# The MLP of the last two batches as 2x2 blocks with seven block products

## The chip, the cores and the metric

The kernel runs on one core of one Trainium2 chip. The metric is the device time of one execution in microseconds; three executions of the kernel before gave a median of 391.68 us (391.42 to 391.88).

## The reference

Attention with one added to the softmax denominator, then an MLP with a squared ReLU, in numpy (cut):

```python
batch, n_heads, seq, head_dim = (8, 12, 448, 64)
scores = scale * np.matmul(q, k.transpose(0, 1, 3, 2))
m = np.max(scores, axis=-1, keepdims=True)
e = np.exp(scores - m)
attn = e / (np.sum(e, axis=-1, keepdims=True) + np.exp(-m) + 1e-09)
attn_out = np.matmul(attn, v)
x = attn_out.transpose(0, 2, 1, 3).reshape(8 * 448, 12 * 64)     # 3584 x 768
h = x @ w_in                                                     # 768 x 2048
r = np.maximum(h, 0.0)
out = (r * r) @ w_out                                            # 2048 x 768, float32
```

Inputs and output are float32; the kernel works in fp16 with float32 sums in PSUM.

## The kernel before

**Layout.** `x` of a batch lies transposed in SBUF as `xts[b]`, six chunks of 128 features by 448 tokens. `win` holds w_in as six chunks of 128 by 2048, `wout` holds w_out as sixteen chunks (`fb`) of 128 by 768. `gs` holds the squared activations, transposed: sixteen blocks of 128 hidden features by a ring of 896 tokens, that is two batches.

**Order.** The kernel writes out the order of every engine's instructions by hand: each engine runs its queue in the order in which the Python code issues it. The string `ORDER` does the first four batches' attention and the beginnings of the MLP, the string `CYCLE` (L750) is run twice, for `b` = 4 and 6 (L774). A run with `b` = 6 does the attention of batches 6 and 7 and, between its steps, the MLP of batches 4 and 5 that lags behind. In these strings `s` computes scores, `e` their exponentials on ScalarE, `a` sums of exponentials on VectorE, `S` the denominators on TensorE, `Z` and `M` their reciprocals on ScalarE, `v` the product with the values, `X` (`quad_x`, L482) the scaled result into `xts`; `o` is a part of an output tile (`out_piece`), `O` and `Q` its two reads from PSUM on VectorE or ScalarE and the store on SyncE's queue; `d` issues DMAs on POOL's and SP's queues.

**PSUM.** Two pools matter: `s_psum` (L61) has two tiles named `sp` of `[128, 2, 512]` float32, each two banks; the ring (`mp_tile`, L86) has four tiles named `mp` of one bank each. The tile framework adds semaphore waits so that a write into a tile comes after the reads of it that were issued earlier, and a read after the writes.

**The last stage**, after the two cycles, is a plain loop. For each of the batches 6 and 7 and each of 16 blocks of hidden features, `tile_in` (L781) issues six matmuls of 128x448 into one `mp` tile, one read with ReLU on VectorE (L505) and one square on VectorE into `gs` (L509). Then `tile_out` (L787) does the output of their 896 tokens, 128 tokens by 384 columns at a time: sixteen matmuls into one `mp` tile, one scaled read on ScalarE (L575) and the store. The last 384 columns are done as 256 and 128.

Of the kernel before, what the change touches and what calls it, by code (L numbers as in the profile page):

```python
# [16 lines left out]
def kernel(  # L17
# [62 lines left out]
    vns, qks, xts, naturals, stages = {}, {}, {}, {}, {}  # L80
# [5 lines left out]
    def mp_tile(dtype=FP32):  # L86
        return ring[-1].tile([128, 512 if dtype == FP32 else 1024], dtype, name="mp")
# [4 lines left out]
    def mm(out_, lhsT, rhs, start, stop):  # L92
        return nc.tensor.matmul(out_, lhsT, rhs, start=start, stop=stop)  # L93
# [69 lines left out]
    def transposed_load(b, i):  # L163
        qk = qk_of(b)
        n, x, c = PLANES[i]
        nc.sync.dma_start(
            out=qk[:, i, 0:c],
            in_=stages[n, b][x:x + c * 2 * D].rearrange("(r c) -> r c", c=2 * D),
            transpose=True,
        )  # L170
# [329 lines left out]
    def relu(hp, key, m, act):  # L500
        rt = rts[key] = r_pool.tile([128, 512], FP16, name="rt")
        if act:
            nc.scalar.activation(out=rt[:, 0:m], in_=hp[:, 0:m], func=AF.Relu)  # L503
        else:
            nc.vector.tensor_scalar(out=rt[:, 0:m], in0=hp[:, 0:m], scalar1=0.0, scalar2=None, op0=ALU.max)  # L505

    def squared(key, t0, n, f0, per):
        r = rts.pop(key)[:, 0:per * n].rearrange("p (j n) -> p j n", j=per)
        nc.vector.tensor_mul(gs[:, f0:f0 + per, t0 % RING:t0 % RING + n], r, r)  # L509
# [3 lines left out]
    def later_in(b, f0, c0, c1, cols=False):  # L513
        if c0 == 0:
            hps[b, "all", f0] = mp_tile()
        hp, xt = hps[b, "all", f0], xts[b]
        for dc in range(c0, c1):
            product(hp[:, 0:S], win[:, dc, f0 * 128:(f0 + 1) * 128], xt[:, dc, :],
                    start=(dc == 0), stop=(dc == DCH - 1), cols=cols)

    def later_relu(b, f0, act):
        relu(hps.pop((b, "all", f0)), (b, "all", f0), S, act)

    def later_squared(b, f0):
        squared((b, "all", f0), S * b, S, f0, 1)
# [69 lines left out]
    raw = load_first_quad()  # L595
# [113 lines left out]

    def period(b):
        m = NQ * (b - 1)
        first = EARLY + 2 * KC * (b - FIRST_PERIOD) // 2

        def following(n):
            ahead, what = ((1, n) if n < 6 else (2, 6) if n < 7 else (1, 6) if n < 8 else (2, n - 8))
            t = b + ahead
            if t < B and (n != 7 or b > FIRST_PERIOD):
                if what < 3:  # L720
                    transposed_load(t, what)
                elif what < 5:
                    tail_keys(t, (what - 2,))
                elif what == 5:
# [7 lines left out]
        return {  # L732
            "s": lambda x, c: quad_scores(m + x, c),
            "e": lambda x, c: quad_exp(m + x, c),
            "a": lambda x, step: add_quad(m + x, step),
            "S": lambda x: sums_of_quad(m + x),
            "Z": lambda x: quad_z(m + x),
            "M": lambda x: quad_reciprocal(m + x),
            "v": lambda x, c: values_step(m + x, c),
            "X": lambda x: quad_x(m + x),  # L740
            "j": lambda n, c0, c1: later_in(*block(n), c0, c1, True),
            "k": lambda n, act: later_relu(*block(n), act),
            "l": lambda n: later_squared(*block(n)),
            "o": lambda n, f0, f1: out_piece(128 * ((first + n) // 2), HALF * ((first + n) % 2), HALF, range(f0, f1), True),
            "O": lambda n, act: out_first(128 * ((first + n) // 2), HALF * ((first + n) % 2), HALF, act),
            "Q": lambda n: out_second(128 * ((first + n) // 2), HALF * ((first + n) % 2), HALF),
            "d": lambda n: following(n),
        }

    CYCLE = """  # L750
# [11 lines left out]
        v0,5 M0 v0,6 s2,2 s2,4 o5,0,2 o5,2,4 o5,4,6 o5,6,8 e2,2 a1,0 o5,8,10 s2,0 e2,4 X0 a1,1 e2,0 o5,10,12 o5,12,14 s3,1 o5,14,16 e3,1 o6,0,2 a1,2  # L762
        a2,0 s3,4 o6,2,4 o6,4,6 O5,0 e3,4 o6,6,8 Q5 s2,5 o6,8,10 o6,10,12 s1,6 e2,5 o6,12,14 e1,6 o6,14,16 a2,1 s3,2 a1,3 o4,0,2 d3 o4,2,4 o4,4,6
        e3,2 s2,6 e2,6 O6,0 o4,6,8 S1 a2,2 Z1 o4,8,10 Q6 o4,10,12 a2,3 o4,12,14 o4,14,16 s3,5 v1,0 O4,0 Q4 v1,1 M1 v1,2 v1,3 v1,4 e3,5 v1,5 v1,6 S2
        v2,0 Z2 v2,1 v2,2 v2,3 v2,4 v2,5 v2,6 X1 M2 o7,0,2 s4,3 e4,3 s3,3 o7,2,4 o7,4,6 X2 e3,3 o7,6,8 o7,8,10 o7,10,12 o7,12,14 o7,14,16 O7,0 Q7 s3,0
        s4,2 e3,0 o8,0,2 o8,2,4 o8,4,6 a3,0 o8,6,8 s3,6 o8,8,10 e4,2 o8,10,12 o8,12,14 e3,6 o9,0,2 s4,1 o8,14,16 s4,0 o9,2,4 O8,0 d10 e4,1 Q8 e4,0
        o9,4,6 o9,6,8 s4,6 o9,8,10 o9,10,12 o9,12,14 s4,4 o9,14,16 e4,6 e4,4 s4,5 d8 o10,0,2 a4,0 o10,2,4 o10,4,6 a3,1 O9,1 d12 a3,2 e4,5 Q9 o10,6,8
        o10,8,10 s5,4 o10,10,12 o10,12,14 s5,1 e5,4 a3,3 o10,14,16 e5,1 a4,1 o12,0,2 O10,0 s5,0 Q10 d9 o12,2,4 d11 e5,0 o12,4,6 s5,5 e5,5 a4,2 o12,6,8
        o12,8,10 o12,10,12 a4,3 s5,3 o11,0,2 o11,2,4 o12,12,14 o12,14,16 e5,3 s5,2 o11,4,6 S3 e5,2 O12,0 o11,6,8 Q12 o11,8,10 o11,10,12 Z3 o11,12,14
        s5,6 o11,14,16 v3,0 O11,1 v3,1 v3,2 v3,3 v3,4 a5,0 v3,5 S4 v3,6 Q11 a5,1 o13,0,2 M3 X3 o13,2,4 o13,4,6 o13,6,8 o13,8,10 o13,10,12 o13,12,14  # L770
        o13,14,16 Z4 a5,2 e5,6 a5,3 O13,1 v4,0 M4 v4,1 v4,2 Q13 v4,3 v4,4 v4,5 v4,6 S5 v5,0 v5,1 v5,2 Z5 M5 v5,3 v5,4 v5,5 X4 v5,6 X5 d13
    """

# [5 lines left out]
    done = EARLY + 2 * KC * (B - FIRST_PERIOD) // 2

    def tile_in(b, f0):  # L781
        for c in range(0, DCH, 2):
            later_in(b, f0, c, c + 2)
        later_relu(b, f0, False)
        later_squared(b, f0)

    def tile_out(tok, n0, w):  # L787
        out_piece(tok, n0, w, range(NFFB))
        out_done(tok, n0, w)

    tiles = [(128 * (n // 2), HALF * (n % 2), HALF) for n in range(done, NT // 64 - 1)]
    tiles += [(NT - 128, HALF, 256), (NT - 128, HALF + 256, 128)]
    for b in (B - 2, B - 1):
        for f0 in range(NFFB):
            tile_in(b, f0)
    for t in tiles:
        tile_out(*t)
# [1 line left out]
_INS = ['q', 'k', 'v', 'moe_w_in', 'moe_w_out']  # L799
_OUTS = [((3584, 768), 'float32')]  # L800
# [25 lines left out]
```

## Time and profile before

| | |
|---|---|
| median of three executions | 391.68 us (391.42 to 391.88) |
| span of the profiled execution, first to last instruction | 389.7 us |
| TensorE, VectorE, ScalarE busy | 382.2, 251.9, 228.4 us |
| last stage: in products | 313.89 to 350.22 us |
| last stage: out products | 350.22 to 386.82 us |
| granted TensorE clock | 1.000 |

No separate time of the profiled execution itself is listed; its span is 2.0 us below the median of the timed ones. In the lines of the profile PE is TensorE, PEld its weight loads, DVE VectorE, ACT ScalarE, POOL GpSimd, SP SyncE; a group reads: line, engine, operation, output <- inputs, shapes, count, then busy time and mean nanoseconds of one, then the idle time in front of them and what ended it. A matmul's mean there is longer than its share of the stream, since consecutive ones overlap; what a matmul costs in a stream is read from windows.

### The profile page before, as it was taken

Reading aid. Unit: us, or ns where it says so; the run is one execution under the profiler, and the core shown is the slowest. Engines: PE = TensorE matmul, PEld = TensorE weight load, DVE = VectorE, ACT = ScalarE, POOL = GpSimd, SP = SyncE. Lnnn points to the kernel's source line nnn. Section 1 sums busy time; section 2 is a strip of 40 time slices with the busy share of each in tenths; the row PEclk is TensorE's granted clock in tenths of the full one; section 3 lists DMA queues with packets and bytes.
Section 4 is the critical chain, followed back from the end, with each engine's and each line's share of the span. In section 5 each row is a group of like instructions: output and inputs, shape, how many; then the busy total and the mean of one; then the engine's idle time right before and its main releaser. Section 6 shows DMA issues by size and latency. Waiting matters only on the chain.

```text
span 389.7 us, 14257 instructions
## 1 busy us (share of the span) xinstructions
PE 382.2 (98%) x6432; PEld 255.2 (65%) x6432; DVE 251.9 (65%) x468; ACT 228.4 (59%) x308; POOL 61.3 (16%) x96
## 2 busy tenths in 40 slices
PE   9789999999999999999999999999999999999997
PEld 5566656566789765667777655567777755556665
DVE  2987994765666766547958757466878788880000
ACT  5999998586689512259988731248988720001221
POOL 8543420025000603100001241210000000000000
DMA  9999999999939899802229697901112200001132
GB/s 154 203 204 205 200 201 204 189 179 176 213 80 150 180 210 203 92 3 65 44 64 202 139 188 160 148 6 47 61 44 64 64 23 2 0 0 62 61 82 81
DMA packets 75052, 45.34 MB, mean 116 GB/s; under 512 B 47472, under 2 KB 72944, under 8 KB 74992
## 3 DMA queue, kind: packets, MB, share of 16 engines
q0 software_dynamic: 24752, 22.62, 37.5%
q1 hardware_dynamic: 49952, 21.59, 27.9%
q8 instruction: 50, 0.82, 0.9%
q10 hardware_dynamic: 288, 0.23, 0.2%
q14 instruction: 10, 0.08, 0.1%
HBM read 45.69 MB, written 17.93 MB: 163 GB/s over the span
## 4 chain that ended last, share of the span: by engine, by line
PE 93%; ACT 4%; DVE 1%; issue 1%; DVEq 0%; ACTq 0%
PE mp L93 81%; PE sp L93 9%; ACT et L254 3%; PE xp L93 2%; PE mp L207 1%; ACT rcp L372 1%; PE mp L234 0%; DVE qk L217 0%; ACT rcp L365 0%; DVE half L341 0%; DVE half L347 0%; ACT rcp L368 0%; DVE half L343 0%; ACT rt L503 0%; DVE half L345 0%
## 5 line engine op out<-in xcount | busy, mean ns | idle before, releaser
L93 PE MATMUL mp<-wout,gs 64*64 64x384 f16 (+2 forms) x2928 | 165.6, 322 | 0.0
L93 PE MATMUL mp<-xt,win 128*64 128x448 f16 (+2 forms) x1188 | 148.3, 347 | 0.1
L93 PEld LDWEIGHTS <-gs 64*64 64x64 f16 (+1 forms) x2928 | 104.3, 106 | 33.6 <-issue 0.2
L93 PEld LDWEIGHTS <-win 128*64 128x64 f16 (+1 forms) x1188 | 83.2, 106 | 63.4 <-issue 4.1
L254 ACT ACTIVATE et<-sp 128x896 f16<-128x896 f32 (+2 forms) x131 | 110.5, 889 | 11.9 <-PE sp L93 11.5
L505 DVE TENSOR_SCALAR rt<-mp 128x448 f16<-128x448 f32 x87 | 54.1, 622 | 16.8 <-PE mp L93 13.8
L509 DVE TENSOR_TENSOR gs<-rt 128x448 f16<-128x448 f16 x128 | 48.3, 395 | 22.1 <-ACT rt L503 20.3
L503 ACT ACTIVATE rt<-mp 128x448 f16<-128x448 f32 x41 | 21.8, 543 | 64.9 <-PE mp L93 55.6
L575 ACT ACTIVATE ot<-mp 128x384 f32<-128x384 f32 (+2 forms) x31 | 14.9, 480 | 70.3 <-PE mp L93 70.0
L93 PE MATMUL sp<-qk 64*64 64x224 f16 (+1 forms) x1056 | 53.9, 274 | 2.2 <-DVE qk L217 0.8
L93 PEld LDWEIGHTS <-qk 64*64 64x64 f16 x1056 | 33.1, 114 | 15.0 <-issue 6.6
L188 POOL COPY flatq<-qk 64x384 f16<-64x384 f16 x20 | 13.8, 690 | 170.8 <-DMA qk<-stage_k 139.5
L254 ACT ACTIVATE nn<-sp 128x896 f16<-128x896 f32 x42 | 37.1, 916 | 4.2 <-PE sp L93 4.2
L487 DVE TENSOR_TENSOR xt<-mp,rcp 128x448 f16<-128x448 f32 x42 | 24.3, 619 | 15.7 <-ACT rcp L466 12.1
L581 DVE SCALAR_TENSOR_TENSOR ot<-mp,ot 128x384 f32<-128x384 f32 x42 | 23.4, 557 | 13.8 <-ACT ot L575 11.3
L93 PEld LDWEIGHTS <-vn 64*64 64x64 f16 x756 | 22.5, 107 | 9.4 <-issue 1.0
L93 PE MATMUL mp<-et,vn 64*64 64x448 f16 (+1 forms) x448 | 24.4, 343 | 0.0
L577 DVE TENSOR_SCALAR ot<-mp 128x384 f32<-128x384 f32 x26 | 14.4, 555 | 15.1 <-PE mp L93 14.9
L463 ACT ACTIVATE rcp<-sp,one_b 128x896 f32<-128x896 f32 x21 | 21.2, 1007 | 3.2 <-PE sp L93 3.1
L466 ACT ACTIVATE rcp<-rcp 128x896 f32<-128x896 f32 x21 | 19.9, 948 | 0.5
L441 DVE TENSOR_TENSOR half<-et 128x1792 f16<-128x1792 f16 x15 | 16.4, 1090 | 4.3 <-ACT et L254 4.2
L443 DVE TENSOR_TENSOR half<-half,et 128x1792 f16<-128x1792 f16 x15 | 16.3, 1087 | 0.3
(59 smaller groups left out, 195.9 us busy)
## 6 DMA issues: line engine op xcount, KB each, us to landing
out_dram<-ot SPq DMA_DIRECT2D x52, 96.0 KB, 2.6
out_dram<-ot SPq DMA_DIRECT2D x19, 192.0 KB, 1.9
win<-in_moe_w_in_dram POOLq DMA_DIRECT2D x8, 384.0 KB, 11.9
wout<-in_moe_w_out_dram POOLq DMA_DIRECT2D x4, 768.0 KB, 15.0
vn<-in_v_dram POOLq DMA_DIRECT2D x10, 288.0 KB, 8.0
stage_q<-in_q_dram POOLq DMA_DIRECT2D x4, 676.0 KB, 11.1
stage_k<-in_k_dram POOLq DMA_DIRECT2D x4, 676.0 KB, 13.8
nn<-in_q_dram POOLq DMA_DIRECT2D x8, 224.0 KB, 8.2
```

Source lines behind the costliest of these rows:

```text
L93: return nc.tensor.matmul(out_, lhsT, rhs, start=start, stop=stop)
L254: nc.scalar.activation(out=out_, in_=in_, func=AF.Exp, scale=scale)
L441: nc.vector.tensor_add(esq[m], a[:, 0:w], a[:, w:2 * w])
L443: nc.vector.tensor_add(esq[m], esq[m], z[:, 0:w])
L463: nc.scalar.activation(out=rcp, in_=zp[:, :, 0:S], func=AF.Ln, bias=one_b)
L466: nc.scalar.activation(out=zqs[m], in_=zqs[m], func=AF.Exp, scale=-1.0)
L487: nc.vector.tensor_mul(xts[b][:, 2 * g + i, :], xqs[m][i][:, 0:S], zqs[m][:, i, :])
L503: nc.scalar.activation(out=rt[:, 0:m], in_=hp[:, 0:m], func=AF.Relu)
L505: nc.vector.tensor_scalar(out=rt[:, 0:m], in0=hp[:, 0:m], scalar1=0.0, scalar2=None, op0=ALU.max)
L509: nc.vector.tensor_mul(gs[:, f0:f0 + per, t0 % RING:t0 % RING + n], r, r)
L575: nc.scalar.activation(out=ot, in_=op[:, 0:w], func=AF.Copy, scale=OUT_SCALE)
L581: nc.vector.scalar_tensor_tensor(out=ot, in0=lo[:, 0:w], scalar=OUT_SCALE, in1=ot, op0=ALU.mult, op1=ALU.add)
```

## The change

Both products of the MLP for batches 6 and 7 are done as products of 2x2 blocks with seven instead of eight block products (Strassen's scheme in Winograd's form). The four quadrants of w_in^T are 8 blocks of 128 hidden features by 3 chunks of 128 inputs; the two columns of the right side are the two batches. For the output, 256 tokens by 768 columns make a group: quadrants of 128 tokens by 1024 hidden features, and of 1024 hidden features by 384 columns. Three groups cover 768 tokens; the last 128 tokens are done as before.

Each scheme needs four sums of quadrants on either side. The sums of w_in (`win_sum`, steps `w0` to `w6`) are put as VectorE instructions of 1536 elements into the last pass of `CYCLE`, behind steps `X2`, `Q7`, `Q8`, `Q9`, `Q10`, `Q12` (`w6`) and `Q11` (`w5`); `w7`, the four sums of x, eight of w_out and eight for each group of `g` follow in the last stage on VectorE. The sums across products are not separate additions: a block product goes on adding to the bank of an earlier one, which is read midway by ScalarE (`kept`, a copy into SBUF), and a later read on VectorE adds the copy. In the first half that later read is a fused add and clamp at zero (`TENSOR_ADD_SAT`).

`CYCLE` differs only in the `w` steps. The core of the rest, issued after the two cycles (cut):

```diff
+    def banks(y):
+        if y % 2:
+            return mp_tile(), mp_tile()
+        sp = s_psum.tile([128, 2, 512], FP32, name="sp")
+        return sp[:, 0], sp[:, 1]
+
+    def kept(src, w, scale_=None):
+        t = slot(w)
...
+            nc.scalar.activation(out=t, in_=src[:, 0:w], func=AF.Copy)
...
+    def relu_add(out_, ps, t):
+        nc.vector._custom_dve(TENSOR_ADD_SAT, out=out_, in0=ps[:, 0:S], in1=t, s0=3.0e38, s1=0.0)
+
+    def onto(out_, lhsT, rhs, begins, first, last):
+        nc.tensor.matmul(out_, lhsT=lhsT, rhs=rhs, start=begins and first, stop=last, skip_group_check=not begins)
...
+    def in_product(f, i):
+        if i == 1:
+            groups[f] = {"xy": banks(f // 2)}
+        g = groups[f]
+        X, Y = g["xy"]
+        for c in range(HC):
...
+            out_, w, x, begins = {
+                1: (X, raw(0, 0), x0[:, c], True), 2: (Y, raw(0, 1), x0[:, HC + c], True),
+                6: (X, win_part(2, f, c) if i == 6 else None, xsum[2][:, c], False),
+                5: (Y, win_part(1, f, c) if i == 5 else None, xsum[1][:, c], True),
+                7: (X, win_part(3, f, c) if i == 7 else None, xsum[3][:, c], False),
+                3: (Y, win_part(4, f, c) if i == 3 else None, x1[:, HC + c], False),
+                4: (X, raw(1, 1), xsum[4][:, c], False)}[i]
+            onto(out_[:, 0:S], w, x, begins, first, last)
+        gf = gs[:, f]
+        if i == 1:
+            g["a"] = kept(X, S)
+        elif i == 2:
+            rt = r_pool.tile([128, 512], FP16, name="rt")[:, 0:S]
+            relu_add(rt, Y, g["a"])
+            nc.scalar.activation(out=gf[:, 0:S], in_=rt, func=AF.Square)
+        elif i == 6:
+            g["u"] = kept(X, S)
+        elif i == 5:
+            g["p"] = kept(Y, S)
+        elif i == 7:
...
+            relu_add(g["r"][:, 1], X, g["p"])
+        elif i == 3:
+            relu_add(g["r"][:, 0], Y, g["u"])
+            nc.vector.tensor_mul(gs[:, f:f + HF + 1:HF, S:2 * S], g["r"], g["r"])
+        elif i == 4:
...
+            nc.scalar.activation(out=rt, in_=X[:, 0:S], func=AF.Relu)
+            nc.vector.tensor_mul(gs[:, f + HF, 0:S], rt, rt)
...
+    def out_group(p):
+        X, Y = banks(0)
...
+        product(X, g_block(p, 0, 0), wout_block(0, 0), True)
+        a = kept(X, HALF, OUT_SCALE)
+        product(Y, g_block(p, 0, 1), wout_block(1, 0), True)
+        out_tile(t0, 0, Y, a)
+        product(X, gsum[p, 2], osum[2], False)
+        u = kept(X, HALF, OUT_SCALE)
+        product(Y, gsum[p, 1], osum[1], True)
+        d = kept(Y, HALF, OUT_SCALE)
+        product(X, gsum[p, 3], osum[3], False)
+        out_tile(t1, HALF, X, d)
+        product(Y, gsum[p, 4], wout_block(1, 1), False)
+        out_tile(t0, HALF, Y, u)
+        product(X, g_block(p, 1, 1), osum[4], False)
+        out_tile(t1, 0, X)
...
+    in_products((0, 1), 1, 2)
+    combine(xsum[1], x1[:, lo], x0[:, lo], True)
+    combine(xsum[2], x1[:, hi], xsum[1], True)
+    combine(xsum[3], x1[:, hi], x1[:, lo], True)
+    combine(xsum[4], x0[:, hi], xsum[2], True)
+    in_products((2, 3), 1, 2)
+    win_sum(7)
+    in_products((0, 1), 6, 5, 7, 3, 4)
+    wout_sum(0)
+    in_products((2, 3), 6, 5, 7)
+    wout_sum(1)
+    in_products((2, 3), 3, 4)
+    for f in (4, 6):
+        in_products((f, f + 1), 1, 2)
+        wout_sum(f - 2)
+        in_products((f, f + 1), 6, 5)
+        wout_sum(f - 1)
+        in_products((f, f + 1), 7)
+        if f == 6:
+            wout_sum(6)
+        in_products((f, f + 1), 3, 4)
+    wout_sum(7)
+    g_sums(0, 0)
+    g_sums(0, 1)
...
-    for b in (B - 2, B - 1):
-        for f0 in range(NFFB):
-            tile_in(b, f0)
-    for t in tiles:
-        tile_out(*t)
+    tile_out(NT - 128, 0, HALF)
+    out_group(0)
+    for y in range(2):
+        g_sums(1, y)
+    out_group(1)
+    for y in range(2):
+        g_sums(2, y)
+    out_group(2)
+    tile_out(NT - 128, HALF, 256)
+    tile_out(NT - 128, HALF + 256, 128)
```

`in_products(fs, *names)` issues the named products one after the other, each for every `f` in `fs`; `product` in `out_group` issues eight matmuls of 384 columns; `out_tile` reads the bank with a copy added (`scalar_tensor_tensor` on VectorE) or, without a copy, on ScalarE, and stores.

More of the change, by code (lines that the diff above doesn't have):

```diff
@@ L8 @@
 from concourse._compat import with_exitstack
+from concourse.dve_ops import TENSOR_ADD_SAT
 FP32 = mybir.dt.float32
@@ L708, with combine, win_block, win_sum @@
         STEPS[step[0]](*(int(y) for y in step[1:].split(",")))
+    HF, HC, HW = NFFB // 2, DCH // 2, DF // 2
+    LAST = (B - 2, B - 1)
+    wsum = {}
+    def combine(out_, in0, in1, minus):
+        (nc.vector.tensor_sub if minus else nc.vector.tensor_add)(out_, in0, in1)
+    def win_block(r, c):
+        return win[:, HC * c:HC * c + HC, HW * r:HW * r + HW]
+    def win_sum(n):
+        which, half = n // 2 + 1, n % 2
+        n0, w = half * HW // 2, HW // 2
+        if not wsum:
+            t = qk_pool.tile([128, 3, COLS], FP16, name="qk").rearrange("p n x -> p (n x)")
+            whole = HC * HW
+            for y in (1, 2):
+                wsum[y] = t[:, (y - 1) * whole:y * whole].rearrange("p (c f) -> p c f", c=HC)
+            wsum[3] = win_block(1, 0)
+            wsum[4, 0] = t[:, 2 * whole:2 * whole + HC * w].rearrange("p (c f) -> p c f", c=HC)
+        if n == 7:
+            wsum[4, 1] = e_pool.tile([128, RUN * 2 * S], FP16, name="et")[:, 0:HC * w].rearrange("p (c f) -> p c f", c=HC)
+        cut = [[win_block(r, c)[:, :, n0:n0 + w] for c in range(2)] for r in range(2)]
+        if which == 4:
+            combine(wsum[4, half], cut[0][1], wsum[2][:, :, n0:n0 + w], True)
+            return
+        in0, in1, minus = {1: (cut[1][0], cut[1][1], False), 2: (wsum[1][:, :, n0:n0 + w], cut[0][0], True),
+                           3: (cut[0][0], cut[1][0], True)}[which]
+        combine(wsum[which][:, :, n0:n0 + w], in0, in1, minus)
+    def win_part(which, f, c):
+        if which == 4:
+            return wsum[4, f // (HF // 2)][:, c, f % (HF // 2) * 128:f % (HF // 2) * 128 + 128]
+        return wsum[which][:, c, f * 128:f * 128 + 128]
     def period(b):
@@ L747, in period @@
             "d": lambda n: following(n),
+            "w": lambda n: win_sum(n) if b + 2 == B else None,
         }
@@ L764 @@
         e3,2 s2,6 e2,6 O6,0 o4,6,8 S1 a2,2 Z1 o4,8,10 Q6 o4,10,12 a2,3 o4,12,14 o4,14,16 s3,5 v1,0 O4,0 Q4 v1,1 M1 v1,2 v1,3 v1,4 e3,5 v1,5 v1,6 S2
[L765 to L770, printed above, removed]
+        v2,0 Z2 v2,1 v2,2 v2,3 v2,4 v2,5 v2,6 X1 M2 o7,0,2 s4,3 e4,3 s3,3 o7,2,4 o7,4,6 X2 w0 e3,3 o7,6,8 o7,8,10 o7,10,12 o7,12,14 o7,14,16 O7,0 Q7 w1 s3,0
+        s4,2 e3,0 o8,0,2 o8,2,4 o8,4,6 a3,0 o8,6,8 s3,6 o8,8,10 e4,2 o8,10,12 o8,12,14 e3,6 o9,0,2 s4,1 o8,14,16 s4,0 o9,2,4 O8,0 d10 e4,1 Q8 w2 e4,0
+        o9,4,6 o9,6,8 s4,6 o9,8,10 o9,10,12 o9,12,14 s4,4 o9,14,16 e4,6 e4,4 s4,5 d8 o10,0,2 a4,0 o10,2,4 o10,4,6 a3,1 O9,1 d12 a3,2 e4,5 Q9 w3 o10,6,8
+        o10,8,10 s5,4 o10,10,12 o10,12,14 s5,1 e5,4 a3,3 o10,14,16 e5,1 a4,1 o12,0,2 O10,0 s5,0 Q10 w4 d9 o12,2,4 d11 e5,0 o12,4,6 s5,5 e5,5 a4,2 o12,6,8
+        o12,8,10 o12,10,12 a4,3 s5,3 o11,0,2 o11,2,4 o12,12,14 o12,14,16 e5,3 s5,2 o11,4,6 S3 e5,2 O12,0 o11,6,8 Q12 w6 o11,8,10 o11,10,12 Z3 o11,12,14
+        s5,6 o11,14,16 v3,0 O11,1 v3,1 v3,2 v3,3 v3,4 a5,0 v3,5 S4 v3,6 Q11 w5 a5,1 o13,0,2 M3 X3 o13,2,4 o13,4,6 o13,6,8 o13,8,10 o13,10,12 o13,12,14
         o13,14,16 Z4 a5,2 e5,6 a5,3 O13,1 v4,0 M4 v4,1 v4,2 Q13 v4,3 v4,4 v4,5 v4,6 S5 v5,0 v5,1 v5,2 Z5 M5 v5,3 v5,4 v5,5 X4 v5,6 X5 d13
@@ L777 @@
             STEPS[step[0]](*(int(y) for y in step[1:].split(",")))
[L779 to L785, printed above, removed]
+    b0, b1 = LAST
+    TOK0 = b0 * S
+    x0, x1 = xts[b0], xts[b1]
+    lo, hi = slice(0, HC), slice(HC, DCH)
+    xt12 = v_pool.tile([128, 2, NQ, KC, D], FP16, name="vn").rearrange("p j g c d -> p (j g c d)")
+    xt34 = e_pool.tile([128, RUN * 2 * S], FP16, name="et")
@@ new lines, with slot @@
+    xsum = {y: (xt12 if y < 3 else xt34)[:, (y - 1) % 2 * HC * S:((y - 1) % 2 + 1) * HC * S].rearrange("p (c n) -> p c n", c=HC)
+            for y in (1, 2, 3, 4)}
+    scratch = qk_pool.tile([128, 3 * COLS // 2], FP32, name="qk")
+    slots = [0]
+    def slot(w):
+        n = slots[0] = (slots[0] + 1) % 9
+        return scratch[:, n * S:n * S + w]
+    def banks(y):
[3 more added lines that the diff above has]
+        return sp[:, 0], sp[:, 1]
@@ new lines, in kept @@
+    def kept(src, w, scale_=None):
+        t = slot(w)
+        if scale_ is None:
+            nc.scalar.activation(out=t, in_=src[:, 0:w], func=AF.Copy)
+        else:
+            nc.scalar.activation(out=t, in_=src[:, 0:w], func=AF.Copy, scale=scale_)
+        return t
+    def relu_add(out_, ps, t):
+        nc.vector._custom_dve(TENSOR_ADD_SAT, out=out_, in0=ps[:, 0:S], in1=t, s0=3.0e38, s1=0.0)
+    def onto(out_, lhsT, rhs, begins, first, last):
+        nc.tensor.matmul(out_, lhsT=lhsT, rhs=rhs, start=begins and first, stop=last, skip_group_check=not begins)
@@ new lines @@
+    groups = {}
+    def in_product(f, i):
[4 more added lines that the diff above has]
+        for c in range(HC):
+            first, last = c == 0, c == HC - 1
+            raw = lambda r, d: win_block(r, d)[:, c, f * 128:f * 128 + 128]
+            out_, w, x, begins = {
[18 more added lines that the diff above has]
+        elif i == 7:
+            g["r"] = es_pool.tile([128, 4 * S], FP16, name="half")[:, 0:2 * S].rearrange("p (o n) -> p o n", o=2)
+            relu_add(g["r"][:, 1], X, g["p"])
[3 more added lines that the diff above has]
+        elif i == 4:
+            rt = r_pool.tile([128, 512], FP16, name="rt")[:, 0:S]
+            nc.scalar.activation(out=rt, in_=X[:, 0:S], func=AF.Relu)
+            nc.vector.tensor_mul(gs[:, f + HF, 0:S], rt, rt)
@@ new lines, with wout_block, wout_sum @@
+    osum = {}
+    def wout_block(r, n):
+        return wout[:, HF * r:HF * r + HF, HALF * n:HALF * n + HALF]
+    def wout_sum(n):
+        which, half = n // 2 + 1, n % 2
+        if half == 0:
+            t = e_pool.tile([128, RUN * 2 * S], FP16, name="et") if which < 3 else nat.tile([128, RUN * 2 * S], FP16, name=f"nn{which - 3}")
+            osum[which] = t[:, 0:HF * HALF].rearrange("p (f n) -> p f n", f=HF)
+        y = slice(half * HF // 2, half * HF // 2 + HF // 2)
+        in0, in1, minus = {
+            1: (wout_block(0, 1), wout_block(0, 0), True), 2: (wout_block(1, 1), osum[1], True),
+            3: (wout_block(1, 1), wout_block(0, 1), True), 4: (wout_block(1, 0), osum[2] if which == 4 else None, True)}[which]
+        combine(osum[which][:, y], in0[:, y], in1[:, y], minus)
@@ new lines, in g_block, with g_sums @@
+    def g_block(p, r, c):
+        return gs[:, HF * c:HF * c + HF, 256 * p + 128 * r:256 * p + 128 * r + 128]
+    gsum = {}
+    def g_sums(p, half):
+        if "t" not in gsum:
+            gsum["t"] = qk_pool.tile([128, 3, COLS], FP16, name="qk").rearrange("p n x -> p (n x)")
+        w = HF * 128
+        for y, z in ((1, 0), (2, 1), (4, 2)):
+            k = 3 * (p % 2) + z
+            gsum[p, y] = gsum["t"][:, k * w:(k + 1) * w].rearrange("p (f n) -> p f n", f=HF)
+        gsum[p, 3] = g_block(p, 1, 0)
+        y = slice(half * HF // 2, half * HF // 2 + HF // 2)
+        combine(gsum[p, 1][:, y], g_block(p, 1, 0)[:, y], g_block(p, 1, 1)[:, y], False)
+        combine(gsum[p, 2][:, y], gsum[p, 1][:, y], g_block(p, 0, 0)[:, y], True)
+        combine(gsum[p, 3][:, y], g_block(p, 0, 0)[:, y], g_block(p, 1, 0)[:, y], True)
+        combine(gsum[p, 4][:, y], g_block(p, 0, 1)[:, y], gsum[p, 2][:, y], True)
@@ new lines, in out_tile, with product @@
+    def out_tile(tok, n0, src, t=None, act=False):
+        ot = osb_pool.tile([128, HALF], FP32, name="ot")
+        if t is not None:
+            nc.vector.scalar_tensor_tensor(out=ot, in0=src[:, 0:HALF], scalar=OUT_SCALE, in1=t, op0=ALU.mult, op1=ALU.add)
+        else:
+            nc.scalar.activation(out=ot, in_=src[:, 0:HALF], func=AF.Copy, scale=OUT_SCALE)
+        store(tok, ot, n0, n0 + HALF)
+    def out_group(p):
+        X, Y = banks(0)
+        t0, t1 = TOK0 + 256 * p, TOK0 + 256 * p + 128
+        def product(out_, g, w, begins):
+            for f in range(HF):
+                onto(out_[:, 0:HALF], g[:, f], w[:, f], begins, f == 0, f == HF - 1)
+        product(X, g_block(p, 0, 0), wout_block(0, 0), True)
[12 more added lines that the diff above has]
+        out_tile(t1, 0, X)
@@ new lines, in in_products @@
+    def in_products(fs, *names):
+        for i in names:
+            for f in fs:
+                in_product(f, i)
+    in_products((0, 1), 1, 2)
[9 more added lines that the diff above has]
+    wout_sum(1)
@@ L789, in tile_out @@
         out_done(tok, n0, w)
-    tiles = [(128 * (n // 2), HALF * (n % 2), HALF) for n in range(done, NT // 64 - 1)]
-    tiles += [(NT - 128, HALF, 256), (NT - 128, HALF + 256, 128)]
-    for b in (B - 2, B - 1):
-        for f0 in range(NFFB):
-            tile_in(b, f0)
-    for t in tiles:
-        tile_out(*t)
+    tile_out(NT - 128, 0, HALF)
[8 more added lines that the diff above has]
+    tile_out(NT - 128, HALF + 256, 128)
 _INS = ['q', 'k', 'v', 'moe_w_in', 'moe_w_out']
```

## The prediction

> **What bounds it now.** First the page: engine shares and the chain that ended last.
>
> ```profile
> PE 382.2 (98%) x6432; PEld 255.2 (65%) x6432; DVE 251.9 (65%) x468; ACT 228.4 (59%) x308; POOL 61.3 (16%) x96
> ...
> PE   9789999999999999999999999999999999999997
> ...
> DVE  2987994765666766547958757466878788880000
> ACT  5999998586689512259988731248988720001221
> ...
> PE 93%; ACT 4%; DVE 1%; issue 1%; DVEq 0%; ACTq 0%
> ```
>
> TensorE is busy from slice 4 to the end; the last four slices have an idle VectorE. So the end is set by how many matmuls are left, and a matmul removed is worth its stream time as long as nothing makes TensorE wait. Next the windows of the stage that is rewritten, cut at its two halves (columns: PE, PEld, DVE, ACT, POOL, granted clock, DMA):
>
> ```profile
> 313.89:350.22 36.33, 36.33 (x196) 18.80 (x193) 32.19 (x64) 0.79 (x1) 0.00 (x0) 1.00 0.00 1
> 350.22:386.82 36.60, 36.60 (x241) 22.80 (x239) 1.14 (x3) 6.77 (x14) 0.00 (x0) 1.00 0.24 71
> ```
>
> 192 matmuls of 128x448 take 36.33 us (0.189 each). Of the 36.60 us, 13 tiles of sixteen 128x384 matmuls come every 2.60 us (0.1625 each), which leaves 2.80 for the two narrow pieces. Clock 1.00, no gap: 72.93 us, all of it stream time. Last, the durations of the readers of PSUM and of the sums, and from the timeline the two hand-overs:
>
> ```profile
> L505 DVE TENSOR_SCALAR rt<-mp 128x448 f16<-128x448 f32 x87 | 54.1, 622 | 16.8 <-PE mp L93 13.8
> L503 ACT ACTIVATE rt<-mp 128x448 f16<-128x448 f32 x41 | 21.8, 543 | 64.9 <-PE mp L93 55.6
> L487 DVE TENSOR_TENSOR xt<-mp,rcp 128x448 f16<-128x448 f32 x42 | 24.3, 619 | 15.7 <-ACT rcp L466 12.1
> L581 DVE SCALAR_TENSOR_TENSOR ot<-mp,ot 128x384 f32<-128x384 f32 x42 | 23.4, 557 | 13.8 <-ACT ot L575 11.3
> L441 DVE TENSOR_TENSOR half<-et 128x1792 f16<-128x1792 f16 x15 | 16.4, 1090 | 4.3 <-ACT et L254 4.2
> L445 DVE TENSOR_TENSOR half<-half 128x896 f16<-128x896 f16 x21 | 13.2, 631 | 0.2
> ```
>
> ```profile
> 14.10 0.42 DVE L217 COPY qk<-mp 128x512 f16<-128x512 f16 x1 [0.50 <-PE mp L207]
> ...
> 14.58 0.58 PE L93 MATMUL sp<-qk 64*64 64x224 f16 x16 [0.52 <-DVE qk L217]
> ...
> 350.22 36.60 PE L93 MATMUL mp<-wout,gs 128*128 128x384 f16 x240
> 353.02 0.49 ACT L575 ACTIVATE ot<-mp 128x384 f32<-128x384 f32 x1 [38.34 <-PE mp L93]
> ```
>
> A tile that starts at 350.22 has been streamed in at 352.82, and ScalarE begins to read it at 353.02: 0.20 from TensorE to its reader. The copy ends at 14.52 and the matmul that waited starts at 14.58: 0.06 back. So a TensorE that waits for the product just issued to be read loses 0.20 + 0.49 + 0.06 = 0.75 us behind ScalarE (384 columns) and 0.20 + 0.56 + 0.06 = 0.82 behind VectorE.
>
> **Removed.** The instruction lists have 12,866 TensorE rows before and 12,770 after: 48 weight loads and 48 matmuls fewer. 24 are of 448 columns (4.54 us), 24 of 384 (3.90): -8.44 us. Without any wait the stage would take 64.5 us.
>
> **Added: waits on the pair of banks.** A block product is three matmuls (0.57 us) in the first half, eight (1.30 us) in the second. Each is read midway and the bank then goes on, so the order alternates X and Y to give the reader time. But where banks() hands out an s_psum tile, X and Y are the two halves of one tile, and the changed program's instruction list shows waits for the whole tile. Of the first output group (TensorE, first matmul of products 2 to 7):
>
> ```
> Matmult sp_8062<-wout_103,gs_104 128x384 [waits Activation_49]
> Matmult sp_8062<-et_7904,qk_8033 128x384 [waits DVE_49]
> Matmult sp_8062<-et_7831,qk_8033 128x384 [waits Activation_49]
> Matmult sp_8062<-nn0_7979,gs_104 128x384 [waits Activation_49]
> Matmult sp_8062<-wout_103,qk_8033 128x384 [waits DVE_49]
> Matmult sp_8062<-nn1_8008,gs_104 128x384 [waits DVE_49]
> ```
>
> Counting the semaphores, product 2 (into Y) waits for ScalarE's copy of product 1 (out of X), the next (into X) for VectorE's read of product 2 (out of Y), and so on: each waits for the read of the product just before it. Nothing on TensorE lies between. Per group three ScalarE and three VectorE reads: 3 x 0.75 + 3 x 0.82 = 4.7 us; the next group has another tile and starts freely. Three groups: **+14.1 us**.
>
> In the first half, pairs f = 2,3 and 6,7 use four separate ring tiles, with three products (1.70 us) between a product and its bank's next use: no stall. Pairs 0,1 and 4,5 use s_psum tiles, and only the other f's product (0.57) lies between. After products 1, 6 and 5 ScalarE's read costs 0.20 + 0.54 + 0.06 - 0.57 = 0.23, after 2, 7 and 3 VectorE's 0.20 + 0.62 + 0.06 - 0.57 = 0.31; before the second read of product 3 stands the square of the first (896 elements, 0.63 by L445, with 0.03 for its own wait): 0.65 more. That is 2.3 us a pair. For 4,5 two wout sums queue among VectorE's reads and add 0.6. For 0,1 the wait for product 6's copy is long: the x sums need the last xt block (1.75 us into the stage); behind it VectorE has two reads (0.57 each, back to back), four x sums (1344 elements, between L445 and L441: 0.86, here 0.83 in a row) and the reads of f = 2,3, to 7.5 us; ScalarE's queue holds two squares for those reads ahead of the copy, which so ends at 8.8, where TensorE was ready at 6.2: +2.6, less the 0.2 already counted. In all 2.3 + 2.4 + 2.3 + 0.6 = **+7.6 us**.
>
> At the seam the last squares reach gs late: VectorE's third wout sum of the last pair stands ahead of them, and the first output tile reads them in its eighth step: +0.8. The eight sums of g (about 0.42 each) that follow end before the products that need them, under that tile and two products; those of the next groups (3.4 us) under the last product of one group and the first two of the next with their gap (4.7 us). So the stage takes 64.5 + 14.1 + 7.6 + 0.8 = 87.0 us against 72.9: +14.1.
>
> **Added: seven w sums in the last cycle.** 1536 elements each, 0.95 by L441 and L445, 0.87 back to back: 6.1 us in VectorE's queue between 289.9 and 313.7 us, where it idles 5.7. The gaps do not all lie where the sums do. Laid into that queue, the second read of tile 10 ends at 303.5, and tile 11, which takes its banks at 303.0, starts 0.55 late; then tile 13 behind Q11 0.2, v4 behind X3 0.45, v5 behind Q13 0.2: **+1.4 us** (ends: 0 and 6.1). POOL's and SP's queues get nothing new: as many stores, closer together.
>
> **Unknown costs.** The fused add and clamp (24 of them, two fp32 inputs, one in PSUM) has no row. Nearest are L505 and L487, 0.62. Ends: 0.39 (L509, same elements, fp16 from SBUF) and 1.24 (two such passes); queues laid out with these give 404 and 421 us. Sums over cut rows: if they ran at L487's 1.04 ns per element instead of L441's 0.6, +12 us; but L341 (cut rows of the same size) has 620 ns beside L445's 631, so I take L441's rate.
>
> Sum: +14.1 + 1.4 = +15.5. The profiled execution's span of 389.7 becomes 405.2; the median of 391.68 lies 2.0 above that span, and I keep the 2.0: **407.2 us**.
>
> **Rivals.** (1) *The waits don't bind*: the reader is done before TensorE gets there, as if each bank stood alone. With the same queues that leaves a stage of 67.5 us (only the x sums' wait, 1.9, the seam and small ones): -5.4 + 1.4 = -4.0, **387.7 us**. It decides once all the waits on banks together fall below 8.4 - 0.8 - 1.4 = 6.2 us, where I reckon 21.7; a copy alone, 0.49 us, is twice what each of the 18 gaps could then be. [...] The semaphores are in the program all the same.
>
> (2) *VectorE sets the pace*: its work in the stage is 50 us by the rows, against 87. With the fused operation at 0.8 us the time is 411, at 1.24 it is 421.
>
> (3) *The clock falls.* All windows before show 1.00, but TensorE had no gaps; in the output groups it would be idle 0.8 us out of every 2.1. At half clock the 27.3 us of group products double: **434 us**. [...] No gap here comes near the longest one reckoned above, 2.6 us, more than once, so I give it little.
>
> **Numbers.** A measurement of this kernel tells about 0.2% from no change. Forecast 0.80 (404 to 411), rival 2 0.10, rival 3 0.05, rival 1 0.04, and 0.01 for no change. The range runs from 403.5 (cheap fused reads, no loss in the cycle) to 413 (half of rival 2). Faster 0.04, same 0.01, slower 0.95.
>
> **What would show it.** Right: from about 315 us TensorE's idle time in front of products into sp, some 22 us, released by ScalarE's copies and VectorE's reads in turn, in even steps of 0.75 and 0.82 in the output groups, and none in front of pair 2,3's later products; clock 1.00; fused reads near 0.62. Wrong: an unbroken TensorE row in the groups (rival 1), VectorE without idle time there (rival 2), a granted clock under 1 (rival 3).

## The result, and the profile after

The changed kernel takes 408.53 us (median of 4 runs, 407.62 to 408.71), the kernel before 391.78 beside it (391.42 to 391.99): the ratio is 1.0423 [1.0409, 1.0438], so the kernel is slower by 4.2%. The forecast was 407.2, range 403.5 to 413.0. The profiled execution took 407.62 us with a span of 405.6, against a forecast span of 405.2; the other three had spans of 406.5 to 406.8 and a mean granted clock of 0.995 or 0.996 where the profiled one had 1.000 (the last section returns to this).

From the page of the changed kernel: the engine shares, the 40 slices of TensorE, VectorE and ScalarE, and the chain that ended last by engine.

```profile
PE 380.6 (94%) x6384; PEld 252.5 (62%) x6384; DVE 272.5 (67%) x497; ACT 249.2 (61%) x348; POOL 61.8 (15%) x96
...
PE   9789999999999999999999999999999798977675
...
DVE  3887993677567575668787575659899868863221
ACT  6999998594886412489887412499986645521011
...
PE 81%; DVE 8%; ACT 7%; issue 3%; DVEq 0%; ACTq 0%
```

There are 48 matmuls fewer, as promised, but the last nine slices of TensorE's row, which were full but for the very last, are at five to nine tenths, and VectorE and ScalarE, 1% and 4% of the chain before, now hold 8% and 7%. In the last four slices, all of them output, neither is busy: VectorE's row ends 3, 2, 2, 1 and ScalarE's 1, 0, 1, 1. TensorE waits there for engines that have time to spare, so it is delay and not load. In the first half of the stage VectorE has less to spare, 30.1 us of 39.3, as the first line of the next table shows.

The windows of the last stage's two halves and of the first and third output group (start and end, length, then busy time of PE, PEld, DVE, ACT and POOL, granted clock, DMA share, GB/s):

```profile
315.46:354.73 39.27, 34.10 (x170) 16.34 (x169) 30.12 (x49) 20.44 (x40) 0.00 (x0) 1.00 0.00 1
354.73:402.81 48.08, 35.93 (x218) 20.23 (x215) 16.98 (x40) 7.61 (x17) 0.00 (x0) 1.00 0.17 52
358.23:372.08 13.85, 10.06 (x58) 5.44 (x56) 5.79 (x15) 1.97 (x4) 0.00 (x0) 1.00 0.17 56
...
386.00:399.97 13.97, 10.06 (x58) 5.44 (x57) 3.21 (x8) 1.97 (x4) 0.00 (x0) 1.00 0.19 56
```

The stage lasts 87.3 us instead of 72.9. Each group holds 56 matmuls of 0.1625, 9.10 us, and takes 13.85 to 13.97 (the second, not shown, 13.92): 4.75 to 4.87 us of it are gaps, 14.4 in the three. VectorE is busy 3.2 to 5.8 us of 14.

Where the gaps lie, by the timeline of the first output group (start, busy time, engine, line, operation and tiles, and in brackets the idle time before it and what ended it):

```profile
364.48 1.46 PE L851 MATMUL sp<-et,qk 128*128 128x384 f16 x8 [0.58 <-ACT qk L844]
365.97 0.49 ACT L844 ACTIVATE qk<-sp 128x384 f32<-128x384 f32 x1 [1.55 <-PE sp L851]
366.51 1.46 PE L851 MATMUL sp<-nn,gs 128*128 128x384 f16 x8 [0.58 <-ACT qk L844]
...
368.07 0.56 DVE L932 SCALAR_TENSOR_TENSOR ot<-sp,qk 128x384 f32<-128x384 f32 x1 [5.68 <-PE sp L851]
368.68 1.46 PE L851 MATMUL sp<-wout,qk 128*128 128x384 f16 x8 [0.70 <-DVE ot L932]
```

Product, read, product, read: no two overlap. Eight matmuls stream 1.30 us; the row says 1.46, since the profile models the end of the last one 0.16 later, so of the predicted 0.75 behind a ScalarE read 0.16 counts as busy and 0.58 as idle. From 364.48 to 366.51 are 2.03 us, 1.30 plus 0.73.

And what TensorE waited for in the last stage, by releaser (total us, times, longest; three lines of 2.0 us together are left out):

```profile
PE sp L851 <- DVE ot L932: 6.2, 9, 0.7
PE sp L851 <- ACT qk L844: 5.4, 9, 0.6
PE sp L851 <- ACT qk L842: 2.6, 2, 2.3
...
PE mp L94 <- DVE gs L887: 0.6, 1, 0.6
```

Nine waits for VectorE's reads and nine for ScalarE's: the 18 gaps. All but the seam's 0.6 are in front of products into `sp`, the two-bank tile. (The seam is where the in products end and the first output tile begins.) With the lines left out these idle times add up to 16.2 us, where the prediction named some 22: the up to 0.16 of each wait that counts as busy is not in them. Against the stream, by the windows, the in products lose 39.3 - 31.8 = 7.5 us and the groups 14.4, together 21.9.

### The profile page after: what moved, and what is told of

It is laid out like the page before. It is cut to its first block, busy times and chain, and to the rows that moved or that the text cites. A ratio compares the mean times of both kernels' runs of the same rounds, so it can differ in the third digit from the quotient of the medians.

```text
span 405.6 us, 14272 instructions
## 1 busy us (share of the span) xinstructions
PE 380.6 (94%) x6384; PEld 252.5 (62%) x6384; DVE 272.5 (67%) x497; ACT 249.2 (61%) x348; POOL 61.8 (15%) x96
## 4 chain that ended last, share of the span: by engine, by line
PE 81%; DVE 8%; ACT 7%; issue 3%; DVEq 0%; ACTq 0%
PE mp L94 60%; PE sp L851 8%; PE sp L94 8%; ACT et L255 3%; DVE half L848 2%; PE mp L851 2%; PE xp L94 1%; DVE ot L932 1%; PE mp L208 1%; ACT qk L844 1%; DVE gs L887 1%; ACT qk L842 1%; ACT gs L877 1%; ACT rcp L373 1%; DVE et L718 0%
## 5 line engine op out<-in xcount | busy, mean ns | idle before, releaser
L94 PE MATMUL mp<-wout,gs 64*64 64x384 f16 (+1 forms) x2736 | 135.5, 322 | 0.7 <-DVE gs L887 0.6
L94 PE MATMUL mp<-xt,win 128*64 128x448 f16 (+2 forms) x996 | 111.8, 346 | 0.1
L94 PEld LDWEIGHTS <-gs 64*64 64x64 f16 (+1 forms) x2736 | 87.6, 107 | 21.4 <-issue 1.3
L94 PEld LDWEIGHTS <-win 128*64 128x64 f16 (+1 forms) x996 | 64.5, 107 | 45.8 <-issue 3.8
L504 ACT ACTIVATE rt<-mp 128x448 f16<-128x448 f32 x41 | 21.9, 543 | 64.8 <-PE mp L94 55.4
L510 DVE TENSOR_TENSOR gs<-rt 128x448 f16<-128x448 f16 x96 | 36.0, 399 | 20.9 <-ACT rt L504 20.1
L506 DVE TENSOR_SCALAR rt<-mp 128x448 f16<-128x448 f32 x55 | 34.1, 622 | 14.3 <-PE mp L94 13.8
L189 POOL COPY flatq<-qk 64x384 f16<-64x384 f16 x20 | 14.3, 717 | 168.2 <-DMA qk<-stage_k 154.5
L94 PEld LDWEIGHTS <-vn 64*64 64x64 f16 x756 | 23.8, 107 | 9.0 <-issue 1.6
L851 PEld LDWEIGHTS <-qk 128*128 128x128 f16 x132 | 12.8, 97 | 22.0 <-issue 12.8
L932 DVE SCALAR_TENSOR_TENSOR ot<-sp,qk 128x384 f32<-128x384 f32 x9 | 5.0, 558 | 26.6 <-PE sp L851 21.8
L578 DVE TENSOR_SCALAR ot<-mp 128x384 f32<-128x384 f32 x26 | 14.4, 554 | 12.0 <-PE mp L94 11.9
```

Source lines behind the costliest of these rows:

```text
L578: nc.vector.tensor_scalar(out=ot, in0=op[:, 0:w], scalar1=OUT_SCALE, scalar2=None, op0=ALU.mult)
L851: nc.tensor.matmul(out_, lhsT=lhsT, rhs=rhs, start=begins and first, stop=last, skip_group_check=not begins)
```

## The experiments

**One part undone: X and Y of the output groups apart.** Only the tiles of the groups are changed; instructions and order stay.

```diff
     def out_group(p):
-        X, Y = banks(0)
+        X, Y = banks(1)
```

> The changed kernel, but each output group takes X and Y as two one-bank tiles of the ring instead of the two halves of an s_psum tile; the first half of the stage is left as it is. Theory (waits on the whole tile): the 18 gaps of the output groups, 14.1 us by the forecast and 3 x 4.75 in the trace after, go; 408.5 - 14.2 = 394.3 us, and the groups run at 9.1 us each. Rival A (a midway read costs TensorE its hand-over whatever the tiles): nothing or little goes, 405 or more. Rival B (VectorE or ScalarE sets the pace): under 4 us goes, as both are idle for more than half of that stretch already.

Measured: 394.22 us (10 runs), ratio 1.0055 [1.0042, 1.0069], 14.3 below the changed kernel. The waits for the groups' reads are gone from the list, and those of the first half stand unchanged. The load on VectorE and ScalarE is the same, so in the groups the second rival (VectorE sets the pace) is out.

**Both parts undone: every X and Y in a tile of its own bank.** The cycle's PSUM pools are closed before the last stage; four one-bank tiles and a ring of four take the place of its two tiles of two banks and its ring of four.

```diff
+    cycle_psum.close()
+    single = ctx.enter_context(tc.tile_pool(name="single", bufs=4, space=bass.MemoryType.PSUM))
+    ring.append(ctx.enter_context(tc.tile_pool(name="last", bufs=4, space=bass.MemoryType.PSUM)))
...
-        sp = s_psum.tile([128, 2, 512], FP32, name="sp")
-        return sp[:, 0], sp[:, 1]
+        return single.tile([128, 512], FP32, name="one"), single.tile([128, 512], FP32, name="one")
```

> The changed kernel, but before the last stage the PSUM pools are closed and eight one-bank tiles opened, so that X and Y are always tiles of their own, in both halves. Theory: all waits on a sibling bank go, 21.7 us by the forecast; the queues laid out with the rows leave a stage of 67.5 us and 387.7 us in all, 4 us under the kernel before. What stays is a stall of about 1.5 us before the third product of the first pair (ScalarE's squares stand ahead of its copies), 0.3 before its second, 0.8 at the seam. Rival A: 405 or more. Rival B (VectorE is the bound as soon as the waits are gone: its work in the first half is some 35 us against TensorE's 31.8): 392 or more.

Measured: 387.64 us (4 runs), ratio 0.9891 [0.9869, 0.9913]: 1.1% faster than before, and within 0.1 us of the 387.7 that the first rival was given. Against the kernel before beside it, 391.95 here, that is a gain of 4.3 us for the rival's 4.0, so part of the 0.1 is luck. The group that had gaps, in this kernel's timeline:

```profile
358.13 1.46 PE L854 MATMUL one<-nn,gs 128*128 128x384 f16 x8
359.43 1.46 PE L854 MATMUL one<-wout,qk 128*128 128x384 f16 x8
```

A product every 1.30 us, no bracket: the read of one product passes under the next. Between this kernel and the one with only the groups apart lie the first half's waits: spans of 385.4 to 385.8 against 390.9 to 391.1 in the executions at a clock of 1.000, 5.4 us; the prediction had 7.6 + 0.8 with pairs and 3.0 without, a difference of 5.4.

**One part alone: the w sums in the last cycle.** The kernel before with the seven sums in the written order; the third goes to a spare place, and nothing reads any of them.

> The kernel before with the seven sums of w_in alone added to VectorE's queue in the last cycle, at the places where the change has them; nothing reads them, and the third sum is written to a spare place instead of over w_in. Theory: they push back the reads that free PSUM banks in that cycle, +1.4 us by the forecast, +1.6 by the trace after (the last stage starts at 315.46 instead of 313.89): 393.3 us. Rival: VectorE's idle time takes them, 391.8 us. Other rival: all of it is on the path, +6 us.

Measured: 393.12 us (12 runs) against 391.95 (23 runs), ratio 1.0019 [1.0008, 1.0031]: 0.7 us by the ratio, 1.2 by the medians. The profiled execution's chain shows one place (start, duration, what), first this kernel and then the kernel before:

```profile
300.33 0.95 DVE qk L717
301.27 0.54 DVE half L447
301.81 1.00 DVE half L443
...
303.38 0.57 DVE ot L581
...
304.00 1.43 PE mp L93 x29
```

```profile
303.19 1.30 PE mp L93 x32
```

A w sum of 0.95 us stands in VectorE's queue ahead of two sums of exponentials and the reads of an output tile, and TensorE goes on 0.05 after the second read: the tile that the prediction named. This execution was 0.51 late from its first stages on, as its rows at 261 us show (261.71 for 261.20), so 0.3 us is lost here, 1.0 in all by 314 us, and 1.2 by the start of the in products (315.62 for 313.89). The other places are told apart below, in the changed kernel's trace.

**One cost doubled, with the waits in place.** The changed kernel with each copy of the output groups made twice, on an engine that is idle most of that time (ScalarE is busy 1.97 of 13.85 us in the changed kernel's first group).

```diff
         a = kept(X, HALF, OUT_SCALE)
+        kept(X, HALF, OUT_SCALE)
...
         u = kept(X, HALF, OUT_SCALE)
+        kept(X, HALF, OUT_SCALE)
...
         d = kept(Y, HALF, OUT_SCALE)
+        kept(Y, HALF, OUT_SCALE)
```

> The changed kernel with each of the nine ScalarE copies of the output groups made twice, the second into a spare slot that nothing reads. Theory: the next product waits for the last read of the tile, so each second copy lengthens its gap by about 0.45 us: 408.5 + 4.0 = 412.6 us. Rival (the gaps are not made by the reads, or ScalarE's idle time takes them): no change.

Measured: 412.24 us (4 runs), ratio 1.0510 [1.0489, 1.0532], 3.7 above the changed kernel (3.4 by the ratios). Two copies take 0.87 us together for 0.49, and the gap grows by as much:

```profile
365.55 0.87 ACT L844 ACTIVATE qk<-sp 128x384 f32<-128x384 f32 x2 [3.71 <-PE sp L851]
366.48 1.46 PE L851 MATMUL sp<-et,qk 128*128 128x384 f16 x8 [0.96 <-ACT qk L844]
```

0.96 for 0.58, nine times, is 3.4 of the 3.7 us. What is added to these reads is added to the kernel.

**The same cost doubled, with the waits taken away.** The kernel with all tiles apart and the same three added lines.

> All X and Y in tiles of their own, and each of the nine ScalarE copies of the output groups made twice, as in the run that doubled them with paired tiles. Theory: with one product (1.30 us) between a read and its bank's next use, 0.20 + 0.49 + 0.45 + 0.06 = 1.20 us still fits, so the second copies cost nothing: 387.6 us as without them, against +4 us with paired tiles. Rival (a longer read is paid for in any case, through ScalarE's queue or the hand-over): +4 us, 391.6.

Measured: 388.29 us (4 runs), ratio 0.9893 [0.9875, 0.9911], where without the second copies it was 0.9891. The same nine copies that cost 3.7 us cost nothing that can be told. TensorE's waits are those of the kernel without them (1.2, 0.6 and 0.2 us).

**What is left, taken away.** Tiles apart, and two moves: the first two products of f = 2,3 go ahead of the third and fourth x sum, and the square of the fourth product goes from VectorE to ScalarE, to shorten the wait at the seam.

```diff
+    in_products((2, 3), 1, 2)
     combine(xsum[3], x1[:, hi], x1[:, lo], True)
     combine(xsum[4], x0[:, hi], xsum[2], True)
-    in_products((2, 3), 1, 2)
...
-            nc.vector.tensor_mul(gs[:, f + HF, 0:S], rt, rt)
+            nc.scalar.activation(out=gs[:, f + HF, 0:S], in_=rt, func=AF.Square)
```

> All X and Y in tiles of their own, and two moves: the products 1 and 2 of the blocks f = 2,3 with their reads are issued between the second and the third sum of x, so that ScalarE's squares no longer hold up its copies of the first pair; and the square after product 4 goes from VectorE to ScalarE. Theory: TensorE's stall in the first pair falls from 1.4 us to 0.3, the seam's stays about 0.8 to 1; the rows laid out give a stage of 66.2 us: 386.5 us. Rival (the stage is paced by VectorE's sums by now): 387.6, as without the moves.

Measured: 387.16 us (4 runs), ratio 0.9874 [0.9858, 0.9891]. The wait of 1.2 us is gone, that at the seam is not: 0.6 as before.

```profile
PE mp L95 <- DVE gs L890: 0.6, 1, 0.6
```

L890 is not the square that was moved, the one after the fourth product, but the one after the third: the second move was made in the wrong place. The rows are shown with the seam, below.

This is the fastest of all, 5.0 us below the 392.19 of the kernel before beside it, though its interval overlaps that of the version without the two moves.

**The w sums on GpSimd.** The fastest version with the eight w sums moved to the engine that does nothing in that part.

```diff
+    def combine_w(out_, in0, in1, minus):
+        (nc.gpsimd.tensor_sub if minus else nc.gpsimd.tensor_add)(out_, in0, in1)
```

> As the run before in this list, and the eight sums of w_in are done by GpSimd instead of VectorE. Theory: GpSimd has nothing else to do there, VectorE's queue in the last cycle is as in the kernel before, and the 1.2 to 1.6 us that the sums cost there come back: 385.1 us. A row for the sums on GpSimd is missing; by its copies (64x384 in 0.69 us, 1.8 ns per element) one takes 2.8 us and seven 19, which fit between 289 and 316 us. Rival A: they take over 4 us each, then the products that need them wait, 388 or more. Rival B: VectorE's own operations get longer while GpSimd works, and the gain is lost.

Measured: 397.5 us (4 runs), ratio 1.0128 [1.0111, 1.0145]: my expectation fell, by 12 us, and its rival B, that VectorE's own operations get longer, is what came. GpSimd takes 3.1 to 3.9 us for a sum that takes VectorE 0.95, and meanwhile VectorE's own work gets longer. Groups between 280 and 325 us (busy us, mean ns, idle before), and the longest of TensorE's waits:

```profile
L447 DVE TENSOR_TENSOR half<-half 128x896 f16<-128x896 f16 x4 | 7.1, 1769 | 0.0
L583 DVE SCALAR_TENSOR_TENSOR ot<-mp,ot 128x384 f32<-128x384 f32 x10 | 5.5, 555 | 1.4 <-ACT ot L577 0.8
...
L725 POOL TENSOR_TENSOR win<-win 128x1536 f16<-128x1536 f16 x2 | 7.9, 3942 | 0.0
```

```profile
PE mp L95 <- DVE ot L583: 6.7, 2, 6.4
```

And the same two groups in the kernel without this move:

```profile
L447 DVE TENSOR_TENSOR half<-half 128x896 f16<-128x896 f16 x4 | 2.5, 617 | 0.0
L583 DVE SCALAR_TENSOR_TENSOR ot<-mp,ot 128x384 f32<-128x384 f32 x10 | 5.5, 554 | 0.6
```

So the sums with both inputs in SBUF at L447 lasted almost three times as long, 1769 ns for 617, and those with an input in PSUM at L583 were untouched, 555 ns for 554. The 6.4 us of TensorE's wait end with such a read from PSUM, which stood behind the longer sums.

**The long wait of the first half alone.** The changed kernel, pairs and all, with only the first of the two moves.

> The changed kernel with paired tiles as it is; only the products 1 and 2 of the blocks f = 2,3 are issued between the second and the third sum of x. Theory: the long wait in the first pair (2.3 us in the trace after, ScalarE's copies behind its squares behind four sums) shrinks by about 1.2 us, and with no idle stretch over 2 us left the granted clock stays at 1.000 in all executions, where three of four of the changed kernel's had 0.995 or 0.996 and took 0.9 us more: 408.5 - 1.2 - 0.9 = 406.4 us. Rival (the low clock has nothing to do with that wait): 407.3 us, and clocks of 0.996 in most executions.

Measured: 406.03 us (4 runs), ratio 1.0357 [1.0339, 1.0374], 2.5 below the changed kernel. The wait in front of the first pair's third product, first in the changed kernel with what ScalarE did ahead of it, then here:

```profile
322.71 1.11 ACT L877 ACTIVATE gs<-rt 128x448 f16<-128x448 f16 x2 [2.29 <-DVE rt L848]
...
324.30 1.29 PE L851 MATMUL sp<-vn,qk 128*128 128x448 f16 x6 [2.35 <-ACT qk L842]
```

```profile
323.84 1.29 PE L851 MATMUL sp<-vn,qk 128*128 128x448 f16 x6 [0.81 <-ACT qk L842]
```

ScalarE's copy stands behind two squares, and these wait for VectorE, which has the x sums ahead of them: the chain that the prediction laid out. Ordered otherwise, 1.54 us of it go. The other 1.0 us goes with the clock: here three of four executions kept 1.000, of the changed kernel's one of four.

## Why the prediction was right, step by step

- **Groups, +14.1.** Measured +14.4 by the windows, and 14.3 by the version with the groups' tiles apart. From product to product the gaps behind ScalarE are 0.73 to 0.80 us, those behind VectorE 0.81 to 0.87, for 0.75 and 0.82. The step that carried it was reading from the instruction list for which read each product waits; the time per gap is 0.20 + read + 0.06, as taken from the kernel before.
- **First half, +7.6.** Products in 39.27 us, against 31.8 + 7.6 = 39.4. The long wait was 2.35 us for a predicted 2.6. By the starts of the pairs' rows (315.46, 336.08, 346.85, and 354.73 for the output) blocks 0 to 3 lost 4.7 us for a predicted 4.7, blocks 4 and 5 lost 2.8 for 2.9, and 6 and 7, on ring tiles, nothing, so the parts are right and not only their sum.
- **Seam, +0.8.** 0.56 idle and the 0.16 that counts as busy, 0.7. The changed kernel's rows show what holds it:

```profile
353.37 0.95 DVE L718 TENSOR_TENSOR nn<-wout,et 128x1536 f16<-128x1536 f16 x1
354.23 0.62 DVE L848 CUSTOM_DVE_ANT_0 half<-mp,qk 128x448 f16<-128x448 f32 x1
...
356.08 0.62 DVE L887 TENSOR_TENSOR gs<-half 128x896 f16<-128x896 f16 x1
...
356.76 1.64 PE L94 MATMUL mp<-wout,gs 128*128 128x384 f16 x9 [0.56 <-DVE gs L887]
```

  TensorE has seven matmuls of the tile behind it and goes on 0.06 us after the square of the third product of f = 7 ends; the third wout sum stands in VectorE's queue ahead of that product's read, as the prediction has it. The move of the square after the fourth product to ScalarE left the wait at 0.6, since this step does not read that square. Whether the wait goes without the wout sum was not run.
- **Cycle, +1.4.** A little less: the stage began 1.57 later than before, of which 0.34 was there at 261 us already, ahead of the sums; 1.2 remain, and the sums alone gave 1.2 by medians and by the start of the in products in the trace. The same rows of TensorE behind each of the four places that the prediction named, first before and then after:

```profile
304.31 0.36 PE L93 MATMUL sp<-qk 64*64 64x224 f16 x8
...
310.95 1.50 PE L93 MATMUL mp<-et,vn 64*64 64x448 f16 x28
...
312.27 0.36 PE L93 MATMUL sp<-half,ones 64*64 64x448 f16 x4
...
313.89 11.34 PE L93 MATMUL mp<-xt,win 128*128 128x448 f16 x59
```

```profile
305.00 0.41 PE L94 MATMUL sp<-qk 64*64 64x224 f16 x5
...
311.82 1.97 PE L94 MATMUL mp<-et,vn 64*64 64x448 f16 x28
...
313.55 0.44 PE L94 MATMUL sp<-half,ones 64*64 64x448 f16 x4
...
315.46 2.72 PE L851 MATMUL sp<-xt,win 128*128 128x448 f16 x12
```

  They are 0.69, 0.87, 1.28 and 1.57 later, so behind tile 11, tile 13, v4 and v5 another 0.35, 0.18, 0.41 and 0.29 us are lost. Predicted were 0.55, 0.2, 0.45 and 0.2: the places are right, and tile 11 was put too high.
- **Unknown rates.** The fused add and clamp is right at the value taken, and so are the sums over cut rows at L441's rate (950 ns for 1536 elements). The row of the fused operation, by group:

```profile
L848 DVE CUSTOM_DVE_ANT_0 half<-sp,qk 128x448 f16<-128x448 f32 x8 | 4.9, 622 | 4.5 <-PE sp L851 4.5
```

- **The rest, 1.3 us of median.** The profiled execution was 0.4 above the forecast, about the 0.34 with which its run began late. The other 0.9 goes with the lower clock in three of four executions, which no term of the sum held. The four terms miss by +0.3, -0.1, -0.1 and -0.2 and so all but cancel; that their sum is closer than each of them is luck.
- **Rivals.** The first (the waits don't bind) was wrong for this kernel and right to 0.3 us of gain for the one with tiles apart: its price was sound, and its condition, that each bank stands alone, is what that experiment made. (Its break-even of 6.2 us over 18 gaps is 0.34 us each, so that the copy's 0.49 is 1.4 times that and not twice; the conclusion is the same.) The second fell with the fused rate and with the idle VectorE. The third expected the clock to fall in the output groups; it stayed at 1.00 in all three windows of the profile, with an idle of 0.58 to 0.70 us in every 2.03 to 2.17. That gaps this short leave the clock alone, the ground for its low chance, was the author's estimate, and half clock stands in no window of the kernel before. The clock did fall in profiles of other kernels, to 0.50 in a window of one, but not in the groups (1.00 in the three windows from 359 to 402 us with doubled copies; last section).

## What to carry to other kernels

When a product is to go on in a bank that is read midway, ask what object the wait is for: with X and Y as halves of one tile, the alternation that was to hide each read bought nothing, and the same instructions in separate tiles turned a loss of 4.2% into a gain of 1.1%. Look up in the instruction list which earlier read each wait names, and price a gap as hand-over plus read plus hand-over (here 0.20 + 0.49 + 0.06 us); the gaps were gone where another product that lasts longer (1.30 us in the output groups) stood between a read and its bank's next use. Work saved on the engine that sets the end is worth its stream time only after the sums and copies that pay for it are found a place; an idle engine is not a free one: with the w sums on GpSimd, sums on VectorE with both inputs in SBUF took 1769 ns for 617 (L447), and the kernel 397.5 us for 387.16.

## What the runs showed of the hardware that was not expected

Behind a wait of TensorE two profiles show a lower granted clock: 0.50 and 0.67 in two windows of 2 us behind an idle of 2.34 us, 0.89 and 0.77 in the windows of 10 us with and behind a wait of 6.4 us. The first is that of the kernel with doubled copies, in windows of 2 us after the long wait of the first pair (the clock is the third figure from the end):

```profile
322.00:324.00 2.00, 0.00 (x0) 0.00 (x0) 2.00 (x4) 1.31 (x3) 0.00 (x0) 0.98 0.00 0
324.00:326.00 2.00, 1.72 (x5) 0.71 (x5) 0.06 (x1) 1.07 (x3) 0.00 (x0) 0.50 0.00 0
326.00:328.00 2.00, 2.00 (x8) 0.90 (x7) 0.23 (x1) 0.69 (x2) 0.00 (x0) 0.67 0.00 0
```

TensorE is idle for 2.34 us up to about 324, then works at a clock of 0.50 up to 326 and of 0.67 up to 328; from 328 on the clock is 1.00 again. The second is that of the kernel with the sums on GpSimd, where TensorE's wait of 6.4 us leaves it 3.63 us busy of the first 10:

```profile
300.00:310.00 10.00, 3.63 (x97) 2.98 (x92) 9.97 (x5) 3.74 (x5) 8.71 (x3) 0.89 0.06 20
310.00:320.00 10.00, 10.00 (x208) 8.57 (x204) 6.35 (x11) 5.92 (x8) 0.00 (x0) 0.77 0.19 62
```

From 320 us on it is 1.00 again. All four executions of that kernel show a mean of 0.991. The changed kernel's profiled execution had the same wait of 2.3 us and kept 1.00, so the idle does not always do it. A mean clock of 0.995 or 0.996 stands in three of its four executions, in eight of ten with the groups' tiles apart, and in all four with doubled copies, at a cost of about 0.9 us (408.53 against 407.62). With the wait at 0.81 us one of four had it, and there the dip lay at 5 to 40 us (0.95 in the windows 5 to 20 and 20 to 40), far from this stage. That the wait is the cause in the executions without a trace is inferred from these counts; two of four of the fastest version show clocks of 0.996 and 0.991 as well, without any such wait in its profile, and two of the 23 executions of the kernel before beside the first four experiments show 0.995 and 0.996, so there are other occasions too.
